# Gated linear attention and a GELU layer on one core: more load buffers, two more pairs through the crossbar, and one dependency in the planner

## The chip, the cores and the metric

The kernel runs on one core of a Trainium2 chip. TensorE multiplies matrices, VectorE (DVE) and ScalarE (ACT) work on elements, GpSimd (POOL) issues the loads here, and SyncE (SP) issues the first loads, the transposes by DMA and the stores. A transpose by DMA goes through the DMA's crossbar and is called that below. The metric is device time in microseconds (us), as the median over runs.

## The reference

For each batch and head (4 batches, 8 heads, 768 tokens, 48 numbers to a head) a state of 48 x 48 is carried over the tokens, and the result goes through a layer with a GELU:

```python
for t in range(S):
    state = alpha[:, :, t, :, None] * state + np.einsum('bhd,bhe->bhde', k[:, :, t], v[:, :, t])
    y[:, :, t] = np.einsum('bhd,bhde->bhe', q[:, :, t], state)
...
x = np.ascontiguousarray(attn_out.transpose(0, 2, 1, 3)).reshape(B * S, H * D)
...
h = x @ w_in                       # 3072 x 384 by 384 x 2048
g = 0.5 * h * (1.0 + np.tanh(c * (h + 0.044715 * h * h * h)))
return (g @ w_out).astype(np.float32)      # 2048 x 384
```

Inputs and output are float32.

## The kernel before

**Tiles.** The tokens are cut into 6 chunks of 128. A chunk of two batches is a *pair*; there are 12, counted here from 0, so pair m is chunk m // 2 and batches 0 and 1 (m even) or 2 and 3 (m odd). The "third pair" of the change is pair 2, the seventh is pair 6, the eighth is pair 7.

**The attention of a pair.** ACT takes the logarithm of alpha (`la`, L294 and L296); TensorE sums it over the tokens with a triangular matrix (`cum`, L313; the sums of the whole chunk, L315); ACT makes `b` = exp(cum), `binv` = exp(-cum) and `bend` from the chunk's sums (L336, L342). DVE makes q' = q·b and k' = k·binv (`qp`, `kp`, L353). q' and k' are transposed into `qkT`: in pairs 0 to 7 on TensorE (L363) with an eviction by DVE or ACT (L381), in pairs 8 to 11 by two crossbar transposes on SP's queue (L401). From `qkT` TensorE makes the products of queries with keys (`at`, L424), DVE masks them (`atm`, L431), and TensorE makes `yps` from the old state (L478) and from `atm` and v (L481). The state takes up k'ᵀv (`kv`, L441; DVE, L463 and L466).

**Between the two halves.** `yps` is copied to `x` by ACT or DVE (L488), and x is transposed into `xT`: in pairs 0 to 6 on TensorE (L495) with a copy by DVE (L499), in pairs 7 to 11 by one crossbar transpose to a batch on SP's queue (L407). There is one `xT` tile to each chunk, six in all.

**The layer.** Block m takes the tokens of pair m: eight steps of first products (`hT`, L507, 6 matmuls each), each followed by a GELU on ACT (L513), then eight groups of second products (`acc`, L526, 4 matmuls each), a copy to `ot` (L538) and a store from SP's queue (L544). These products are one stream with a fixed order; the attention of later pairs is put between them. The logarithms of a pair wait for the last GELU of an earlier block (the table `DECAYS`: pairs 6 and 7 follow block 4, pair 8 follows block 5), because ACT has to load another function table for them.

**What sets the order.** A planner (`Scheduler`) knows every piece of work as a task with a cost, a priority, the tasks it depends on and the buffers it takes. It takes the engine that can go on first, and of that engine's tasks that can start within 60 ns of the earliest the one with the lowest priority number, until all are placed; the instructions are written in that order, and each engine runs its own in order. Attention tasks have lower numbers than the stream, so the stream fills what is left. Where the planner sees TensorE idle for over 300 ns in its first 60 us, it puts in filler products that compute nothing (`idle`, L224). A DMA transpose on SP costs 1.25 us of SP in its table (`turn`) and counts as landed 2.2 us later (`landed`); transposes and stores are counted as one queue (`xbar`). Waits on the chip are set from the tiles that instructions read and write, whatever the planner assumed.

**Buffers.** A task that takes a buffer waits until the users of the one it follows in the ring are done. `BUFS` has 4 load buffers for alpha (`a`), 4 for `q`, 4 for `k`, 2 for float32 v of pairs 0 and 1 (`v`) and 6 for bfloat16 v (`vb`). Loads are issued by POOL in the order of `LOADS` unless a buffer holds one back: weights first, then a, q, k, v of pair after pair. The tag `ca` has one PSUM tile, which `cum` and part of `at` take in turn.

**Pair 2** is worked in two halves (`SPLIT`), one batch each: `parts` gives it two `cum` tasks, whose sums lie in one `ca` tile, and two sets of `b`, `binv`, `bend`. The list `exps` holds these six in order.

Of the kernel before, what the change touches and what calls it, by code (L numbers as in the profile page):

```python
# [5 lines left out]
BF16 = mybir.dt.bfloat16  # L6
F16 = mybir.dt.float16
F32 = mybir.dt.float32
# [128 lines left out]
class _Kernel:  # L137
# [10 lines left out]
             ('a', 1, 0, 1), ('a', 1, 1, 2), ('q', 1, 0, 1), ('k', 1, 0, 1), ('q', 1, 1, 2), ('k', 1, 1, 2))  # L148
    NARROW = (0, 1)

    TURN_QK, TURN_X = (8, 9, 10, 11), (7, 8, 9, 10, 11)

    EV_ACT = (0, 1, 2, 3)

# [1 line left out]

    URGENT = (2,)
    BUFS = dict(ca=1, yk=2, ff=4, la=3, qp=4, kp=4, b8=2, kn=2, qkT=4, atm=6, x=3, ot=5, bend=3, ends=8,
                a=4, q=4, k=4, v=2, vb=6)

    def __init__(self, ctx, tc, q, k, v, alpha, w_in, w_out, out):
        nc = self.nc = tc.nc
        self.tc, self.out = tc, out
        B, H, S, D = q.shape
        self.B, self.H, self.S, self.D = B, H, S, D
        C = self.C = 128
        self.NCH = S // C
        self.src = {"a": alpha, "q": q, "k": k, "v": v}
        self.w_in_dram, self.w_out_dram = w_in, w_out
        self.d_model, self.d_ff = w_in.shape  # L170
        self.NKT, self.NFT = self.d_model // C, self.d_ff // C

        self.const = ctx.enter_context(tc.tile_pool(name="const", bufs=1))
        self.sb = ctx.enter_context(tc.tile_pool(name="sb", bufs=1))
        self.ps = ctx.enter_context(tc.tile_pool(name="ps", bufs=1, space=bass.MemoryType.PSUM))

        const = self.const
        self.ut_h = const.tile([C, C], F16, name="ut_h")
        self.ut = const.tile([C, C], BF16, name="ut")
        self.gate = const.tile([C, 1], F32, name="gate")  # L180
        self.ut_blk = [const.tile([C, C], F16, name=f"ut_blk{i}") for i in range(2)]
        self.blk = const.tile([C, 4], F16, name="blk")
        self.ident = const.tile([C, C], BF16, name="ident")
        self.ones = const.tile([C, 1], F16, name="ones")
        self.zero = const.tile([C, 512], BF16, name="zero")
        self.w_in = [const.tile([C, self.NKT, self.d_ff // 4], BF16, name=f"w_in{i}") for i in range(4)]
        self.w_out = const.tile([C, self.NFT, self.d_model], BF16, name="w_out")
        self.half = const.tile([C, 2], F32, name="half")
        self.state = [[const.tile([C, H // 2, 2 * D], BF16, name=f"st{b}_{i}") for i in range(2)]
                      for b in range(B)]  # L190
        self.ring = {n: [const.tile([C, 2, H, 64], F16 if n == "la" else BF16, name=f"{n}{i}")
                         for i in range(self.BUFS[n])] for n in ("la", "qp", "kp")}
        self.used = {n: 0 for n in self.ring}
        self.xT = [const.tile([C, self.NKT, B, C], BF16, name=f"xT{c}") for c in range(self.NCH)]
        self.NG = 2
        self.gT = [const.tile([C, self.NFT, B * C], BF16, name=f"gT{i}") for i in range(self.NG)]
        self.eng = {"ACT": nc.scalar, "DVE": nc.vector}
# [30 lines left out]
    def load(self, n, c, i, lo=0, hi=2):  # L228

        nc, C, H, D, R = self.nc, self.C, self.H, self.D, self.R  # L230
        u = self.p[c, i]

        def emit(e):
            t = "vb" if n == "v" and u["m"] not in self.NARROW else n
            if t not in u:
                u[t] = self.tile(t, [C, 2, H, D], BF16 if t == "vb" else F32)
            dma = (nc.sync if e == "SP" else nc.gpsimd).dma_start
            src = self.src[n][2 * i + lo:2 * i + hi]
            if u["packed"] and n != "v":
                dma(u[n][:, lo].rearrange("p (o r) d -> p o (r d)", o=2),  # L240
                    src[0, :, c * C:(c + 1) * C].rearrange("h (g r) d -> g h (r d)", r=R))
            else:
                dma(u[t][:, lo:hi].rearrange("t b h d -> t (b h) d"), src.rearrange("b h s d -> s (b h) d")[c * C:(c + 1) * C])  # L243
        return emit
# [159 lines left out]
        return emit  # L404

    def turn_x_dma(self, u, i, c, b):
        return lambda e: self.nc.sync.dma_start_transpose(self.xT[c][:, :, b, :], u["x", i])  # L407

    def attn(self, u, units, apart):
        nc, H, C = self.nc, self.H, self.C  # L410
# [85 lines left out]
        return emit  # L496

    def turned_x(self, u, i, c, b):
        return lambda e: self.copy(e)(self.xT[c][:, :, b, :], u["xT_ps", i])  # L499

    def layer1(self, f, c, lo, hi, nt):
        def emit(e):
            w_in = self.w_in[nt // 4].rearrange("k j (c r) -> k j r c", r=self.NFT // 4)
            h = f["h", c, lo, nt] = self.tile("ff", [self.C, 2, (hi - lo) * self.C], F32, "hT")
            for s in range(2):
                for j in range(self.NKT):
                    self.nc.tensor.matmul(h[:, s], w_in[:, j, nt % 4 + s],  # L507
                                          self.xT[c][:, j, lo:hi].rearrange("p g t -> p (g t)"),
                                          start=j == 0, stop=j == self.NKT - 1, skip_group_check=True)
        return emit  # L510

# [35 lines left out]
    def tasks(self):  # L547
        s = self.s = Scheduler(self.BUFS, self.fill, 60000)
        B, NCH = self.B, self.NCH
# [5 lines left out]
        loads, n, gate, held = {}, 0, [], {}  # L555
# [26 lines left out]
        for step in self.LOADS:  # L582
            if step[0] == "v":
                rows(int(step[1:]), "v")
            elif step[:4] == "gate":
                r, m, j = step[4:].split()
                m, j = int(m), int(j)
# [11 lines left out]
        for m, (c, i) in enumerate(pairs):  # L599
            u, P = self.p[c, i], 100 * m  # L600
# [3 lines left out]
            cums, exps = [], []  # L604
# [28 lines left out]
            if m in self.CUM_FF:  # L633
                cums[0].take("ff", *exps[:3])
                cums[1].take("ff", *exps[3:])
            else:
                cums[0].take("ca", *exps)
            exps[0].take("b8", *qp, *kp)
            if m == 1:
                cums[1].deps.append(ys[1, 0])  # L640
# [5 lines left out]
            vin = [loads["v", m, j] for j in range(2)]  # L646
# [4 lines left out]
            for j in range(2):  # L651
                o, k = P + 10 + 3 * j, kp[j]
# [27 lines left out]
            for j in range(2):  # L680
                b, o, k, ms, turned = 2 * i + j, P + 10 + 3 * j, kp[j], masks[j], turns[j]
                at = ats[m][-1 if m not in self.SINGLE else j]
                if m in self.NARROW:
                    vin[j].deps += turned
                y = s.add("y", {"PE": W["intra"] + (W["inter"] if c else 0)}, P + 20 + j, self.y(u, j, c, b),
                          ms + turned + [vin[j]] + ([states[b, c - 1]] if c else []))
                xc = s.add("x", {"ACT": W["xc_act"], "DVE": W["xc"]}, P + 20 + j, self.x(u, j), [y])
                if m in self.TURN_X:
                    xe = tx = s.add("turn", {"SP": W["turn"]}, P + 22 + j, self.turn_x_dma(u, j, c, b), [xc], xbar=W["xbar_x"], late=W["late_x"] * (m < 7))
                else:  # L690
                    tx = s.add("tx", {"PE": W["tx"]}, P + 22 + j, self.turn_x(u, j), [xc])
                    xe = s.add("xe", {"DVE": W["xe"]}, P + 22 + j, self.turned_x(u, j, c, b), [tx])
                    tx.take("yk", xe)
                y.take("yk", xc)
                xc.take("x", tx)
                users += [at, y]
                ms[0].take("atm", y)
                xts[c, b], ys[b, c] = xe, y
                vs.append(y)
                if c < NCH - 1:  # L700
                    if u["packed"]:
                        tb = s.add("t", {"PE": W["t4"]}, P + 29 + j, self.turn_back(u, j), turned)
                        k = s.add("ev", {"DVE": W["ev4"], "ACT": W["ev4_act"]}, P + 29 + j, self.turned_back(u, j), [tb])
                        tb.take("yk", k)
                        users.append(tb)
                        backs.append(tb)
                    kv = s.add("kv", {"PE": W["kv"]}, P + 30 + j, self.kv(u, j), [k, vin[j]])
                    st = states[b, c] = s.add("st", {"DVE": W["st" if c else "st0"]}, P + 30 + j, self.carry(u, j, c, b),
                                              [kv, end] + ([states[b, c - 1], ys[b, c - 1]] if c else []))
                    kv.take("yk", st)  # L710
                    vs.append(kv)
                    kvs.append(kv)
                    cs.append(st)
# [9 lines left out]
            qp[0].take("qp", *tq)  # L723
            kp[0].take("kp", *tq, *kvs)
            if m in self.NARROW:
                loads["v", m, 0].take("v", *vin)
                vin[0].take("vb", *vs)
            else:
                loads["v", m, 0].take("vb", *vs)
# [115 lines left out]
```

## Time and profile before

| | |
|---|---|
| median of 7 runs | 181.46 us (181.08 to 182.05) |
| the profiled execution | 181.25 us, of which the profile's span is 179.5 us |
| granted TensorE clock | 0.999 of full speed |
| busy: TensorE, ACT, DVE, POOL | 172.9, 130.9, 96.9, 57.6 us |
| loaded from and written to memory | 25.17 MB and 4.72 MB |

Times inside the profile are counted from the start of the span. A group or a row is named by engine, line and tile, written as out<-in. Matmuls overlap: the duration of one is its way through the array, and what a row of them costs the stream is seen from start to start. A wait is put down to the event that came last. "SPq" is SP issuing a DMA; the transfer itself runs on 16 DMA engines and lands later. The forty digits of a row of the overview are the busy tenths of forty equal slices of the span.

### The profile page before, as it was taken

The page shows a single profiled execution, that of the slowest core. Times are in us where ns is not written, and L with a number is a line of the kernel's source. Part 1 is how long each engine was busy: PE and PEld are TensorE (multiplying, and loading weights), DVE is VectorE, ACT ScalarE, POOL GpSimd, SP SyncE. Part 2 cuts the span into 40 slices and gives each one's busy share as a digit, 9 for nine tenths or more (in the row PEclk, how much of TensorE's full clock was granted, in tenths as well). Part 3 has the DMA queues.
Part 4 walks back from the last instruction along what each step waited for, and adds up shares of the span by engine and source line. Part 5 has one row for each costly group of instructions (what it writes and reads, how often), then busy time and mean ns, then how long its engine had stood idle before and what let it go on. Part 6 is the DMA issues. An engine that isn't in the chain of part 4 may idle for free.

```text
span 179.5 us, 4459 instructions
## 1 busy us (share of the span) xinstructions
PE 172.9 (96%) x1860; PEld 136.4 (76%) x1860; DVE 96.9 (54%) x191; ACT 130.9 (73%) x216; POOL 57.6 (32%) x64
## 2 busy tenths in 40 slices
PE   6979999999999999999999999999999999999993
PEld 2557699566896897798698789689688697796972
DVE  6579850145968794596499798199245415000000
ACT  4669778974898678858888757887987984491831
POOL 2397336996646775722721300000000000000000
PEclk9999999999999999999999999999999999999999
DMA  4999999999999999999993736652361270311102
GB/s 121 277 277 212 209 244 233 215 209 208 221 318 187 224 260 197 188 266 201 173 231 97 165 102 104 106 132 54 68 163 45 62 166 26 90 41 47 44 0 88
DMA packets 45957, 28.14 MB, mean 157 GB/s; under 512 B 34545, under 2 KB 42353, under 8 KB 45937
## 3 DMA queue, kind: packets, MB, share of 16 engines
q0 software_dynamic: 26464, 17.70, 59.4%
q1 hardware_dynamic: 19472, 10.16, 21.9%
q8 instruction: 14, 0.23, 0.6%
q14 instruction: 7, 0.05, 0.1%
HBM read 25.17 MB, written 4.72 MB: 167 GB/s over the span
## 4 chain that ended last, share of the span: by engine, by line
PE 90%; DMA 5%; ACT 1%; DVE 1%; SPq 0%; issue 0%; POOL 0%
PE hT L507 35%; PE acc L526 35%; PE at L424 4%; DMA v<-in_v_dram 3%; PE qkT_ps L363 3%; PE yps L481 3%; PE kv L441 2%; PE cum L313 2%; PE yps L478 2%; DMA a<-in_alpha_dram 2%; PE xT_ps L495 1%; PE idle L224 1%; PE cum L281 1%; PE cum L315 1%; PE k_ps L389 1%; ACT vb L324 1%
## 5 line engine op out<-in xcount | busy, mean ns | idle before, releaser
L507 PE MATMUL hT<-xT,w_in 128*128 128x256 bf16 x576 | 69.3, 273 | 0.0
L526 PE MATMUL acc<-w_out,gT 128*128 128x384 bf16 (+1 forms) x400 | 69.1, 320 | 0.0
L513 ACT ACTIVATE gT<-hT 128x512 bf16<-128x512 f32 x96 | 56.7, 597 | 16.5 <-PE hT L507 12.9
L507 PEld LDWEIGHTS <-w_in 128*128 128x128 bf16 x576 | 61.0, 114 | 1.2
L526 PEld LDWEIGHTS <-gT 128*128 128x128 bf16 x400 | 36.7, 98 | 19.2
L431 DVE TENSOR_TENSOR atm<-at,ut 128x512 bf16<-128x512 f32 x48 | 30.3, 682 | 13.2 <-PE at L424 13.1
L353 DVE TENSOR_TENSOR qp<-q,b 128x768 bf16<-128x768 f32 (+1 forms) x15 | 11.9, 794 | 24.9 <-ACT b L342 23.7
L538 ACT COPY ot<-acc 128x384 f32<-128x384 f32 (+1 forms) x18 | 8.2, 458 | 14.1 <-PE acc L526 11.9
L243 POOL DMA_DIRECT2D q<-in_q_dram x11 | 12.2, 1107 | 14.6 <-DVE xT L499 7.1
L243 POOL DMA_DIRECT2D vb<-in_v_dram x11 | 12.1, 1102 | 12.0 <-PE xT_ps L495 6.3
L243 POOL DMA_DIRECT2D a<-in_alpha_dram x11 | 12.2, 1112 | 4.6 <-DMA q<-in_q_dram 1.4
L243 POOL DMA_DIRECT2D k<-in_k_dram x11 | 12.1, 1104 | 4.5 <-DMA w_out<-in_moe_w_out_dram 2.1
L342 ACT ACTIVATE b<-cum 128x768 bf16<-128x768 f32 (+1 forms) x15 | 10.3, 683 | 3.6 <-PE cum L315 2.5
L215 ACT ACT_TABLE_LOAD x9 | 11.5, 1283 | 0.9 <-PEq L829 0.7
L353 DVE TENSOR_TENSOR kp<-k,binv 128x768 bf16<-128x768 f32 (+1 forms) x15 | 11.9, 791 | 0.3 <-DMA k<-in_k_dram 0.3
L513 ACT ACT_TABLE_LOAD x9 | 11.5, 1283 | 0.2
L342 ACT ACTIVATE binv<-cum 128x768 bf16<-128x768 f32 (+1 forms) x15 | 10.2, 680 | 0.0
L381 DVE COPY qkT<-qkT_ps 128x1024 bf16<-128x1024 bf16 (+1 forms) x13 | 8.6, 685 | 2.7 <-PE qkT_ps L363 2.6
L488 DVE CAST x<-yps 128x384 bf16<-128x384 f32 x11 | 6.1, 558 | 7.0 <-PE yps L481 6.9
L224 PE MATMUL idle<-zero 128*128 128x512 bf16 x26 | 8.5, 436 | 1.2 <-DVE half L798 1.2
L463 DVE TENSOR_TENSOR stmp<-kv,st 128x384 f32<-128x384 f32 x16 | 8.8, 551 | 1.2 <-PE kv L441 1.2
L488 ACT CAST x<-yps 128x384 bf16<-128x384 f32 x13 | 6.2, 475 | 4.4 <-PE yps L481 4.4
(63 smaller groups left out, 164.9 us busy)
## 6 DMA issues: line engine op xcount, KB each, us to landing
out_dram<-ot SPq DMA_DIRECT2D x23, 192.0 KB, 2.3
a<-in_alpha_dram POOLq DMA_DIRECT2D x9, 384.0 KB, 11.5
q<-in_q_dram POOLq DMA_DIRECT2D x9, 384.0 KB, 10.9
k<-in_k_dram POOLq DMA_DIRECT2D x9, 384.0 KB, 11.3
vb<-in_v_dram POOLq DMA_DIRECT2D x9, 192.0 KB, 11.6
w_in<-in_moe_w_in_dram POOLq DMA_DIRECT2D x4, 384.0 KB, 9.5
w_out<-in_moe_w_out_dram POOLq DMA_DIRECT2D x4, 384.0 KB, 11.4
a<-in_alpha_dram SPq DMA_DIRECT2D x4, 192.0 KB, 3.6
```

The source lines that it names most:

```text
L215: nc.scalar.add_instruction(mybir.InstLoadActFuncSet(name=nc.get_next_instruction_name(), act_func_set_id=i, engine=mybir.EngineType.Activ ...
L224: self.nc.tensor.matmul(ps, self.zero[:, 0:self.C], self.zero, start=True, stop=True)
L243: dma(u[t][:, lo:hi].rearrange("t b h d -> t (b h) d"), src.rearrange("b h s d -> s (b h) d")[c * C:(c + 1) * C])
L342: self.nc.scalar.activation(u[n].rearrange("t i h d -> t i (h d)")[:, lo:hi], cum, AF.Exp, scale=1.0 if n == "b" else -1.0)
L353: self.nc.vector.tensor_tensor(out, rows, b, op=ALU.mult)
L381: self.copy(e)(t, ps)
L431: self.nc.vector.tensor_tensor(u["atm", i][:, o], u["at", i][o], self.ut[:, None, :].to_broadcast([self.C, self.H // 2, self.C]), op=ALU.mult)
L463: nc.vector.tensor_tensor(s, acc, old, op=ALU.add)
L488: self.copy(e)(x, u["y", i].rearrange("t h d -> t (h d)"))
L507: self.nc.tensor.matmul(h[:, s], w_in[:, j, nt % 4 + s], self.xT[c][:, j, lo:hi].rearrange("p g t -> p (g t)"), start=j == 0, stop=j == se ...
L513: return lambda e: self.nc.scalar.activation(self.gT[c % self.NG][:, nt:nt + 2, lo * self.C:hi * self.C], f.pop(("h", c, lo, nt)), AF.Gelu ...
L526: self.nc.tensor.matmul(f["acc", c, b][:, lo:hi], self.gT[c % self.NG][:, nt, b * self.C:(b + 1) * self.C], self.w_out[:, nt, lo:hi], star ...
```

## The change

- The crossbar also takes q' and k' of pair 7 (two transposes) and x of pair 6 (two transposes). TensorE's transposes and their evictions are left out there.
- `a` has 6 buffers in place of 4, `q` and `k` have 5 in place of 4. The float32 v of pairs 0 and 1 has no buffers of its own any more and takes two of `a`'s.
- There are three `xT` tiles in place of six, used by chunk c modulo 3.
- In the planner, the second `cum` of pair 2 depends on the first half's `b` and `binv`.
- The extra lateness that the planner gave to an x transposed in a pair before 7 is given before 6; no pair that uses the crossbar is under either bound.

```diff
-    TURN_QK, TURN_X = (8, 9, 10, 11), (7, 8, 9, 10, 11)
+    TURN_QK, TURN_X = (7, 8, 9, 10, 11), (6, 7, 8, 9, 10, 11)
...
-                a=4, q=4, k=4, v=2, vb=6)
+                a=6, q=5, k=5, vb=6)
...
-        self.xT = [const.tile([C, self.NKT, B, C], BF16, name=f"xT{c}") for c in range(self.NCH)]
+        self.NX = 3
+        self.xT = [const.tile([C, self.NKT, B, C], BF16, name=f"xT{c}") for c in range(self.NX)]
...
-                u[t] = self.tile(t, [C, 2, H, D], BF16 if t == "vb" else F32)
+                u[t] = self.tile("a" if t == "v" else t, [C, 2, H, D], BF16 if t == "vb" else F32, t)
...
-        return lambda e: self.nc.sync.dma_start_transpose(self.xT[c][:, :, b, :], u["x", i])
+        return lambda e: self.nc.sync.dma_start_transpose(self.xT[c % self.NX][:, :, b, :], u["x", i])
...
+            if m in self.SPLIT:
+                cums[1].deps += exps[:2]
...
-                    xe = tx = s.add("turn", {"SP": W["turn"]}, P + 22 + j, self.turn_x_dma(u, j, c, b), [xc], xbar=W["xbar_x"], late=W["late_x"] * (m < 7))
+                    xe = tx = s.add("turn", {"SP": W["turn"]}, P + 22 + j, self.turn_x_dma(u, j, c, b), [xc], xbar=W["xbar_x"], late=W["late_x"] * (m < 6))
...
-                loads["v", m, 0].take("v", *vin)
+                loads["v", m, 0].take("a", *vin)
```

The other places that name `xT[c]` (L499, L508) become `xT[c % self.NX]` in the same way.

More of the change, by code (lines that the diff above doesn't have):

```diff
@@ L498, in turned_x @@
     def turned_x(self, u, i, c, b):
-        return lambda e: self.copy(e)(self.xT[c][:, :, b, :], u["xT_ps", i])
+        return lambda e: self.copy(e)(self.xT[c % self.NX][:, :, b, :], u["xT_ps", i])
     def layer1(self, f, c, lo, hi, nt):
@@ L507, in emit @@
                     self.nc.tensor.matmul(h[:, s], w_in[:, j, nt % 4 + s],
-                                          self.xT[c][:, j, lo:hi].rearrange("p g t -> p (g t)"),
+                                          self.xT[c % self.NX][:, j, lo:hi].rearrange("p g t -> p (g t)"),
                                           start=j == 0, stop=j == self.NKT - 1, skip_group_check=True)
```

## The prediction

> **What bounds the kernel now.** I read the shares first, then the chain that ended last, then TensorE's own waits, then its order of time at two places, and last the transfers. Pairs are counted from 0: the eighth pair is pair 7, the seventh pair 6, the third pair 2.
>
> ```profile
> PE 172.9 (96%) x1860; PEld 136.4 (76%) x1860; DVE 96.9 (54%) x191; ACT 130.9 (73%) x216; POOL 57.6 (32%) x64
> PE   6979999999999999999999999999999999999993
> DMA  4999999999999999999993736652361270311102
> PE 90%; DMA 5%; ACT 1%; DVE 1%; SPq 0%; issue 0%; POOL 0%
> ```
>
> TensorE is busy in every slice from the fourth to the last but one, at a granted clock of 0.999. Asked for TensorE's waits from 20 us to the end, the trace has one:
>
> ```profile
> PE cum L313 <- ACT binv L342: 0.3, 1, 0.3
> ```
>
> So a microsecond taken out of TensorE's stream comes off the end, and the one stall is the second. In the order of time it looks so:
>
> ```profile
> 34.57 0.24 PE L315 MATMUL cum<-ones,la 128*128 128x1 f16 x4
> 34.67 0.81 PE L526 MATMUL acc<-w_out,gT 128*128 128x384 bf16 x4
> 35.77 0.32 PE L313 MATMUL cum<-la,ut_h 128*128 128x384 f16 x1 [0.29 <-ACT binv L342]
> ```
>
> Four products `acc` fill 0.65 us (0.162 us start to start), so they end issuing at 35.32; the next instruction starts at 35.77. Counted by starts the hole is 0.45 us (the 0.29 leaves out the modelled tail of the last product). The second sum of pair 2 waits for `binv` of the first half: both halves lie in one `ca` tile, and the planner did not know of that wait.
>
> **The change part by part.** *q', k' of pair 7 by crossbar.* Away go 16 transposes on TensorE; the chain, in order of time, has them at 99.82, and the transposes of pair 6's x just ahead (start, duration, count):
>
> ```profile
> 97.53 0.17 PE xT_ps L495 x3
> ...
> 99.00 0.17 PE xT_ps L495 x3
> ...
> 99.82 0.89 PE qkT_ps L363 x16
> ```
>
> The sixteen are 0.89 us of TensorE; two evictions on DVE (1.29 us at 100.30) go too; no row has another engine held up by them. In come two DMA transposes on SP's queue, each 1.24 us of issue; DVE, ACT and POOL get nothing new.
>
> *x of pair 6 by crossbar.* Away go 2 x 3 transposes, 2 x 0.17 = 0.34 us of TensorE, and two copies on DVE (0.36 each). In come two more SP transposes of 1.24 us. SP has room: between its store issues at 90.27 and 103.14 it issues nothing, and the four need about 5.0 us.
>
> *The order of pair 2's sums.* The planner now puts the second sum after the first half's `b` and `binv`. Worked by hand from its cost table (taken for the order alone), one more `acc` group (0.65 us) goes ahead of the sum and nothing else changes place: the transposes of pair 2 still follow three groups later. The second sum then starts at 35.32 + 0.65 = 35.97, after `binv` has ended at 35.71. The hole of 0.45 us goes. What is late next: the second half's `b`, `binv`, q', k' each move 0.20 later (k' done at 38.02 in place of 37.82); its transposes stood at 38.43 (q) and 38.65 (k) and would come at 37.98 and 38.20. They still find their input, by 0.2 us. Sums, evictions and the first products of block 2 at 47.11 then all follow 0.45 earlier; the copy of x they wait for follows TensorE's order too.
>
> *Buffers.* POOL's loads of q, k, a come up to one or two pairs earlier; v of the first two pairs takes two of the six `a` buffers, as many in all as before (4 + 2), so up to pair 5 the loads keep their order. After that the gain is no time by itself: after 20 us POOL alone waits for loads (a wait of q' on DVE at 58.8 is put down to one, but ended with `b`, at 58.73), and the cover is wide (a of pair 5 landed at 54.2, used at 70.7). What it moves is the end of the load traffic:
>
> ```profile
> 88.74 1.16 POOL L243 DMA_DIRECT2D q<-in_q_dram  x1 [0.58 <-DVE qp L353]
> 89.89 1.15 POOL L243 DMA_DIRECT2D k<-in_k_dram  x1
> 98.11 1.15 POOL L243 DMA_DIRECT2D q<-in_q_dram  x1 [7.07 <-DVE xT L499]
> 99.36 1.15 POOL L243 DMA_DIRECT2D k<-in_k_dram  x1
> ```
>
> The last q and k waited for a buffer until pair 7's q' was made; with five buffers they wait for pair 6's, at about 88 to 89. The loads then run without holes: 24 are to come once v of pair 5 has landed at 59.3; the next 17 landed in 27.4 us, 1.6 each, so they end near 98, where before the load landed at 97.3 was followed by a hole, and by the last two at 102.9 and 104.4. The three `xT` tiles in place of six reuse a tile three chunks later; its readers ended more than 40 us before, cost 0.
>
> *Do the four transposes land in time?* This is the open price. Shifted by the 0.45: first x of pair 6 is ready at 95.33 and issues then; q' is ready at 97.25; the second x (ACT, 97.71) waits behind q' on SP and issues at 98.6; k' (DVE no longer copies x between q' and k': done at 98.2) issues at 99.9, behind it. The nearest rows are the same four kinds in the same order, one pair later:
>
> ```profile
> 107.17 1.28 SPq L407 DMA_TRANSPOSE xT<-x  x1
> 108.56 1.24 SPq L401 DMA_TRANSPOSE qkT<-qp  x1
> 109.89 1.24 SPq L407 DMA_TRANSPOSE xT<-x  x1
> 111.22 1.26 SPq L401 DMA_TRANSPOSE qkT<-kp  x1
> ```
>
> They landed 2.4, 3.5, 4.3 and 3.8 us after issue began. So x lands at 97.8 and 102.9, q' at 100.8, k' at 103.7. Needed: block 6's first product stood at 105.32; less 0.45, less 1.23, less about 0.6 if `at` of pair 7 now comes behind it, it wants x at 103.0; `at` (L424) wants k' about 0.65 later, at 103.7. Both just fit. Anything later stalls TensorE at once: the queue is in order, and behind that product wait the gelus on ACT and all of block 6.
>
> The loads are the unknown. A store on the same queue took 5.3 us at 90.27 with loads in flight, 1.9 to 2.9 at 103 to 107 with few, and 6.2 to 9.5 between 44 and 80. Bounds for the stall: 0 (quiet rows) and 4 us (the second x takes 8.4, the store at 57.92, and lands at 107). It can't be below 0, as TensorE does not wait there now. I take 0.3, near the quiet end: by 98.6 the loads are landed or nearly so, and only the first x meets them.
>
> *Two rules from the skill.* The row: one crossbar transpose of q' carries eight 128x128 blocks and lands in 2.7 us (117 to 121), while its blocks hold TensorE 55 ns each. The Trainium skill, "VectorE: DVE Perf Modes", Rules for kernel authors, says to transpose 128x128 on TensorE where PSUM will do, and its table of three paths has 390 ns there and 1309 ns on the crossbar. Read serially that is an estimate of 22 blocks at 0.92 us more, 20 us lost and a time near 201. Here TensorE is the bound and the crossbar's time lies beside it, so the row decides. Second row: the store of 90.27, 5.3 us. The skill's "DMA: Bandwidth & Descriptors", Queues, rings and completion order, has each DMA engine turn between queues packet by packet; then a transpose would not wait out the loads and the stall would be 0, 1.7 us saved. The row has the store behind loads issued before it; I keep 0.3.
>
> **The sum.** 0.89 + 0.34 + 0.45 - 0.30 = 1.38 us off the profiled execution, 181.25 us (span 179.5 and 1.75 around it), so 179.9; it stands 0.21 under the median of 181.46, which becomes 180.1.
>
> **The rivals.** *Slower: the second x of pair 6 is stuck behind the loads.* Place: block 6's first product. It decides once x lands after 103.0 + 1.68 = 104.7, a latency over 6.1 us from 98.6. For it: stores took 6.2 to 9.5 us under full load, and the added buffers keep the loads going to about 98. Against: by 98.6, when that x issues, the loads have ended by my count. At 8.4 us: 4.0 lost, 1.7 won, 183.8; at 7 us, 182.4.
>
> *No difference.* The same wait at 5.7 to 6.4 us: 1.3 to 2.0 lost, about 181.4.
>
> *Only the transposes count.* The hole at 35 us is refilled: the last gap before block 2 (one filler product at 46.56) shows TensorE was short of work there, and if x of pair 2 keeps its time, 46.76, the 0.45 comes back as filler or wait. Against: that x hangs on TensorE's own order, which moves as a whole. Then 1.23 - 0.3 = 0.93: 180.5.
>
> *The change does more than needed and nothing stalls:* 1.68 off, 179.8; with the lower runs 179.5.
>
> **How the numbers follow.** Forecast (both gains, stall 0 to 0.7: 179.8 to 180.5): 0.60. Only the transposes, or a stall of 0.7 to 1.3 (180.5 to 181.1): 0.20. No difference: 0.09. Slower: 0.11. A measurement tells about 0.2% (0.36 us) from nothing. Faster is the first two, 0.80. The range runs from 179.5 to 181.5; the likeliest case alone 179.5 to 180.5.
>
> **What would show it.** Right: 112 transposes of q', k' on TensorE in place of 128, 36 of x in place of 42; by the crossbar 12 of x in place of 10, and 10 of q', k' in place of 8; no wait of `cum` for `binv`; POOL done before 92; block 6's first product near 103.0. Wrong: a wait of `hT` or `at` for a transfer between 102 and 108, latencies over 5 us there, or new filler products before 47 us, which would mean that the planner's order moved elsewhere too.

## The result, and the profile after

| | before | after |
|---|---|---|
| median | 181.54 us (45 runs) | 180.82 us (17 runs) |
| ratio of after to before | | 0.9952, interval 0.9939 to 0.9966 |
| the profiled execution (its span) | 181.25 us (179.5) | 180.74 us (179.0) |
| first product of block 1 to first product of block 11 | 139.38 us | 138.65 us |

The kernel is faster by 0.72 us, where 1.38 was forecast. The last row of the table is read from the two traces, and it is the measure for all traces below. It leaves out the start, since block 0's first product comes at 16.0 to 16.6 us in most traces and at 18.7 and 18.9 in two. It also leaves out the end, and there the change costs 0.24 us: from block 11's first product to the end of the span it is 13.62 us before and 13.86 after. The work of TensorE in that stretch is the same. The difference comes behind the last store's landing, from where the span goes on for 0.98 us before and 1.21 after. There SP has two semaphore events in the kernel before and six in the kernel after, 0.06 us apart. In all fourteen traces of this case two such events go with 0.96 to 0.98 us, six with 1.21 to 1.23, eight with 1.34 to 1.36.

So the two spans differ by 0.51 us (0.73 less 0.24, and 0.03 at the start), and that the 0.73 of the last row is so near the 0.72 of the medians is in part luck. Lines of the kernel after are numbered one higher than before, and two or three higher towards the end of the file.

The page of the kernel after, in the shares, the tenths and the chain that ended last:

```profile
PE 172.5 (96%) x1838; PEld 135.7 (76%) x1838; DVE 95.1 (53%) x187; ACT 131.3 (73%) x216; POOL 57.8 (32%) x64
...
PE   6999999999999999999999989999999999999992
...
DMA  4999999999999999999999970353270360401102
...
PE 88%; DMA 8%; DVE 1%; ACT 1%; SPq 0%; issue 0%; POOL 0%
```

TensorE has 22 instructions less, as forecast (16 and 6 transposes; 112 and 36 are left). DMA is at 9 for some slices longer and then drops. In the chain its share rose from 5% to 8%, by a line that was not there before: `DMA qkT<-kp`, 3%. TensorE's waits from 20 us to the end say the same; the wait of `cum` for `binv` is gone and another has come:

```profile
PE at L425 <- DMA qkT<-kp: 0.8, 1, 0.8
```

TensorE in order of time, at the two places that the prediction named:

```profile
34.54 0.24 PE L316 MATMUL cum<-ones,la 128*128 128x1 f16 x4
34.64 1.46 PE L527 MATMUL acc<-w_out,gT 128*128 128x384 bf16 x8
35.94 0.33 PE L314 MATMUL cum<-la,ut_h 128*128 128x384 f16 x1
...
103.02 0.82 PE L508 MATMUL hT<-xT,w_in 128*128 128x256 bf16 x6
104.68 0.62 PE L425 MATMUL at<-qkT 64*128 64x128 bf16 x16 [0.84 <-DMA qkT<-kp]
```

Pair 2's second sum starts at 35.94 with no wait. Block 6's first product starts at 103.02; its six matmuls start 0.109 us apart, so the next instruction could start at 103.68, and `at` of pair 7 starts at 104.68. Counted by starts, TensorE stands still for 1.0 us (the 0.84 leaves out the modelled tail). So 0.45 + 0.34 + 0.89 = 1.68 us of work and idling went, and 1.0 came back: 0.68 between block 1 and block 11, where the two traces differ by 0.73. With the 0.24 at the end 0.44 is left.

The four issues on SP, in order of time, are where they were expected:

```profile
95.33 1.27 SPq L408 DMA_TRANSPOSE xT<-x  x1
97.29 1.23 SPq L402 DMA_TRANSPOSE qkT<-qp  x1
98.61 1.21 SPq L408 DMA_TRANSPOSE xT<-x  x1
99.91 1.26 SPq L402 DMA_TRANSPOSE qkT<-kp  x1
```

They landed at 101.0, 101.84, 102.27 and 104.64. POOL issued the last two loads well ahead of them:

```profile
88.80 1.15 POOL L244 DMA_DIRECT2D q<-in_q_dram  x1 [0.66 <-DVE kp L354]
90.71 1.15 POOL L244 DMA_DIRECT2D k<-in_k_dram  x1 [0.76 <-DVE qkT L382]
```

The last load landed at 100.65. The question of the experiments is why k' took 4.73 us after its issue.

**Theory L**, the prediction's: the loads are still in flight and delay what is issued beside them. **Theory F**, the rival, came from the DMA view of the stretch from 102 to 104.6 us (40 slices of 0.065 us: busy tenths and GB/s of all engines; below, the queues with packets, MB and share; the hardware queue carries SP's transposes and stores, the software queue POOL's loads):

```profile
DMA  9999999999900000000000000101011069999989
GB/s 295 268 280 288 532 260 284 268 443 363 189 0 0 0 0 0 0 0 0 0 4 8 8 8 8 12 8 12 8 12 24 0 236 378 378 378 378 378 162 299
...
q1 hardware_dynamic: 909, 0.38, 113.3%
q8 instruction: 1, 0.02, 2.6%
```

No load is left on the software queue here, and yet for some 1.3 us (102.7 to 104.0) nearly nothing moves. Just before, at 102.27, one packet of 16 KB starts on an "instruction" queue and takes 1.09 us: by the queue's name, the core fetches code. The single packets tell more. A transpose of q' or k' here ends with 32 packets of 4 bytes. Of those of k', 30 start between 102.53 and 102.63 and the last two at 103.97. In between, 22 packets of 256 bytes run one after another from 103.345 to 103.947, nearly all at 35 to 56 ns in place of 18, and the first of them starts 14 ns before the fetch ends (103.359). The store's packets, issued behind k', stand from 102.6 to 104.1. So a sixteenth of k' seems to wait until the fetch is through, and all else behind it; that is a reading, which the experiments test. The Trainium skill, "Runtime: NRT & Kernel Launch", section Instruction fetch mechanics, says that code reaches an engine in blocks of 16 KB, 256 instructions, by a DMA queue of its own; the queue of this profile with 14 packets and 0.23 MB fits that size. What such a block does to other transfers, the runs have to show.

### The profile page after: what moved, and what is told of

Read it like the earlier page. It is cut to its first block, busy times and chain, and to the rows that moved or that the text cites. A ratio compares the mean times of both kernels' runs of the same rounds, so it can differ in the third digit from the quotient of the medians.

```text
span 179.0 us, 4421 instructions
## 1 busy us (share of the span) xinstructions
PE 172.5 (96%) x1838; PEld 135.7 (76%) x1838; DVE 95.1 (53%) x187; ACT 131.3 (73%) x216; POOL 57.8 (32%) x64
## 4 chain that ended last, share of the span: by engine, by line
PE 88%; DMA 8%; DVE 1%; ACT 1%; SPq 0%; issue 0%; POOL 0%
PE hT L508 35%; PE acc L527 33%; PE at L425 4%; DMA v<-in_v_dram 3%; PE qkT_ps L364 3%; PE yps L482 3%; DMA qkT<-kp 3%; PE kv L442 2%; PE yps L479 2%; PE cum L314 2%; DMA a<-in_alpha_dram 2%; PE xT_ps L496 1%; PE idle L225 1%; PE cum L282 1%; PE cum L316 1%; PE k_ps L390 1%
## 5 line engine op out<-in xcount | busy, mean ns | idle before, releaser
L508 PE MATMUL hT<-xT,w_in 128*128 128x256 bf16 x576 | 69.0, 273 | 0.0
L508 PEld LDWEIGHTS <-w_in 128*128 128x128 bf16 x576 | 61.1, 113 | 1.2
L467 DVE TENSOR_TENSOR st<-stmp,ends 128x384 bf16<-128x384 f32 x16 | 8.9, 558 | 0.6
```

The source lines that it names most:

```text
L467: nc.vector.tensor_tensor(new.rearrange("f p (o d) -> f (p o) d", o=2), acc.rearrange("f p (o d) -> f (p o) d", o=2), ends, op=ALU.mult)
L508: self.nc.tensor.matmul(h[:, s], w_in[:, j, nt % 4 + s], self.xT[c % self.NX][:, j, lo:hi].rearrange("p g t -> p (g t)"), start=j == 0, st ...
```

## The experiments

### Moving the code fetches

TensorE's filler products at the start of the kernel compute nothing. Written as four products of 128 columns in place of one of 512, they add 78 products early (156 instructions, with their weight loads) and little time, and everything that TensorE fetches later is fetched at another moment. If the fetch makes k' late, k' comes in time; if the loads do, nothing changes.

```diff
-                self.nc.tensor.matmul(ps, self.zero[:, 0:self.C], self.zero, start=True, stop=True)
+                for j in range(4):
+                    self.nc.tensor.matmul(ps[:, j * 128:(j + 1) * 128], self.zero[:, 0:self.C], self.zero[:, 0:128], start=True, stop=True)
```

**After with these fillers:**

> The changed kernel, with each filler product of 512 columns written as four of 128 columns: the same columns, 78 more products, 156 more instructions on TensorE before 47 us. Theory F (instruction fetch): TensorE's code comes in blocks of 16 KB by DMA, one in some 11 us; the one at 102.27 us held one DMA engine for 1.09 us while k' of pair 7 was on the crossbar, and all engines waited, so k' landed at 104.6 and L425 stalled 1.0 us. With 156 instructions more ahead of it the fetch comes about 6.8 us earlier, at 95 to 97, k' lands at about 103.1, the stall is under 0.2 us and the time 0.7 to 1.0 us below the changed kernel's (179.8 to 180.1; ratio to before 0.990 to 0.993). Theory L (loads): the transposes are late because load traffic runs to 100.6; then k' still lands at 104.4 to 104.8, the stall stays at 0.8 to 1.0 us and the time at 180.8.

Measured: 180.35 us, 0.9934 of before (0.9915 to 0.9952); block 1 to block 11 takes 137.75 us, 0.90 less than after. The fetch begins at 95.91, where theory F had put it (95 to 97). k' is issued at 100.47 and lands 2.74 us later, and `at` doesn't wait. The DMA view from 100.4 to 103.3 us has no instruction queue:

```profile
GB/s 106 208 187 226 212 208 138 42 0 1 0 0 0 0 0 0 0 35 159 261 290 290 297 290 293 286 290 282 297 293 195 57 4 106 148 275 339 339 381 360
...
q1 hardware_dynamic: 1556, 0.50, 72.0%
```

k' moves between 101.6 and 102.8 without a break. This speaks for F, with one weakness: in this run the loads ended at 99.4, before k' was issued, while after had them until 100.65.

**Before with these fillers**, as a control:

> Control: the kernel before with the filler products split in four. Nothing on TensorE's path waits for a transfer there, so both theories expect the time of before, ratio 0.9985 to 1.0015. Theory F also expects the fetch of 112.19 to come near 105.4 and the transposes issued at 109.89 and 111.22 to land about 1 us sooner than their 4.3 and 3.8 us; theory L expects them as they were.

Measured: 1.0040 of before (1.0022 to 1.0059), where the expectation was no change: the fillers cost something there, so what they win above isn't their own cheapness. In the profile the fetch that fell at 112.19 moved to 105.7, and the transposes at 109.84 and 111.14, which took 4.3 and 3.8 us in before, took 2.5 and 2.8. But another fetch moved onto 118.4, where q' of pair 9 was under way: it took 3.7 us (2.7 in before), k' was issued behind it at 119.81 in place of 119.44, and `at` waited:

```profile
PE at L425 <- DMA qkT<-kp: 0.2, 1, 0.2
```

From block 1 to block 11 the trace takes 139.62 us, 0.24 more than before. The profiled execution was the fastest of its runs (181.43, the median is 182.36), so what most runs lost beyond that, some 0.5 us of the 0.73 that the ratio gives, is in no trace and stays open.

**The same kernels again**, one profiled execution each, to separate the loads from the fetch: after twice, after with the fillers once more, and with fillers of two products of 256 columns, which should bring the fetch to another moment again.

```diff
-                self.nc.tensor.matmul(ps, self.zero[:, 0:self.C], self.zero, start=True, stop=True)
+                for j in range(2):
+                    self.nc.tensor.matmul(ps[:, j * 256:(j + 1) * 256], self.zero[:, 0:self.C], self.zero[:, 0:256], start=True, stop=True)
```

> The changed kernel itself, a second look at its trace. Theory F (code fetch): the fetch comes at 102.0 to 102.8 counted from a start like the first look's, k' of pair 7 is on the queue then, and L425 waits 0.5 to 1.2 us. Theory L (loads): the wait goes with the landing of the last load: about 1 us if that is at 100.5 or later, none if it is before 99. Theory B (both are needed): a wait only where k' is still being moved when the fetch begins, and that is so where the last load lands late.

> The changed kernel itself, a third look; expected as for the second: F a wait of 0.5 to 1.2 us whatever the loads do, L a wait that goes with the last load's landing alone, B a wait only where k' is still being moved at the fetch.

> The kernel with filler products in four, a second look: its fetch comes at about 96 and the next at about 108. F and B expect no wait of L425 for k' over 0.2 us, even if the last load lands at 100.5 or later; L expects about 1 us in that case.

> The changed kernel with each filler product in two of 256 columns: 52 more instructions on TensorE, a fetch about 2.3 us earlier, at 100, when q' or the second x are on the crossbar. F: they land about 1 us later than without, k' follows at 103.2 to 104.0, and L425 waits 0 to 0.4 us. L: as the changed kernel, by the last load's landing. B: no wait over 0.4 us.

The four executions took 183.22, 181.04, 179.87 and 180.08 us. In the first, block 0's first product came 2.65 us later than in after and the granted clock was 0.50 from 13.6 to 17.0 us, so its total says nothing; from there on the clock is whole and its transfers can be read. The traces, in order of the fetch's place:

| kernel | fetch begins | last load landed | k' issued | k' takes | `at` stands (page's wait) |
|---|---|---|---|---|---|
| after, fillers in four | 95.91 | 99.4 | 100.47 | 2.74 | 0 |
| the same again | 96.77 | 99.76 | 99.94 | 2.80 | 0 |
| after, fillers in two | 100.13 | 98.9 | 100.13 | 3.57 | 0 |
| after | 102.27 | 100.65 | 99.91 | 4.73 | 0.8 |
| after again (second execution) | 102.41 | 100.4 | 100.34 | 4.58 | 0.7 |
| after again (first execution) | 104.43 | 99.87 | 102.57 | 4.53 | 0.7 |

The last row decides. All loads had landed 2.7 us before k' was issued, and k' was still 1.8 us late. The DMA view of that run from 102.5 to 107.2 us (40 slices of 0.118 us) and its wait:

```profile
GB/s 135 224 220 196 48 1 0 0 0 0 13 183 283 292 292 285 423 272 227 53 65 288 118 0 0 0 0 2 9 9 9 9 11 13 144 353 418 292 249 294
...
q1 hardware_dynamic: 1867, 0.62, 86.3%
q8 instruction: 1, 0.02, 1.8%
```

```profile
PE at L425 <- DMA qkT<-kp: 0.7, 1, 0.7
```

It is the same picture as in after, without loads: k' moves at full rate, the rate falls to 0 and then to 9 GB/s, and k' ends late. In the single packets 30 of the 32 end marks start between 104.68 and 104.85 and two at 106.40, and the 22 late packets begin at 105.767, 14 ns before the fetch ends (105.781). The other execution of after has 103.586 and 103.600, again 14 ns. With the fetch elsewhere, in the two executions with fillers in four, all 32 marks start within 0.2 us. So theory L falls as the reason of this wait, and theory B with it, for k' waited here though no load was late. In fillers in two the fetch lies at the beginning of k' and on q' and the second x (4.62 and 3.68 us), and k' lands at 103.71, 0.3 us before `at` starts. Three executions of after with the fetch on k' all wait; three with the fetch moved don't.

Over all fourteen traces of this case, the transposes that were issued after the last load had landed, sorted by whether a packet of an instruction queue was in flight at any time between issue and landing. There are two such queues, one with packets of 16 KB and one with a few of 8 KB:

| | no fetch: number, us from issue to landing | with a fetch: number, us from issue to landing, median |
|---|---|---|
| x, one batch | 63: 2.28 to 2.38 | 79: 2.28 to 4.34, 2.81 |
| q' | 37: 2.70 to 2.79 | 19: 2.75 to 3.96, 3.36 |
| k' | 50: 2.72 to 2.95 | 10: 2.76 to 4.53, 3.36 |

Of 150 transposes without a fetch none is late. With one, some are on time, such as the k' of 2.76 us whose fetch began after its end marks (in the version with room, below).

### The parts, one at a time

**The order of pair 2's sums alone, in before:**

```diff
+            if m in self.SPLIT:
+                cums[1].deps += exps[:2]
```

> The kernel before with the one new dependency of pair 2's second sum alone. The prediction's step: the hole of 0.45 us before the sum goes and nothing comes back, 0.45 us faster (ratio 0.9975), first product of block 2 at 46.65. Rival (the hole is refilled): block 2 starts at 47.1 as before, ratio 1.000.

Measured: 181.13 us, 0.9970 (0.9954 to 0.9986); block 1 to block 11 takes 138.93, 0.45 us less. TensorE in order of time has the eight `acc` products in place of four and no wait:

```profile
34.93 1.46 PE L526 MATMUL acc<-w_out,gT 128*128 128x384 bf16 x8
36.22 0.33 PE L313 MATMUL cum<-la,ut_h 128*128 128x384 f16 x1
```

From block 2 on the distances from block to block are those of before. The hole isn't refilled later: the rival that said so falls.

**The order, the buffers and x of pair 6**, q' and k' of pair 7 staying on TensorE:

```diff
-    TURN_QK, TURN_X = (7, 8, 9, 10, 11), (6, 7, 8, 9, 10, 11)
+    TURN_QK, TURN_X = (8, 9, 10, 11), (6, 7, 8, 9, 10, 11)
```

> The changed kernel with q', k' of pair 7 back on TensorE; x of pair 6 by crossbar, buffers and order kept. By the terms of the sum 0.45 + 0.34 = 0.79 us below before with no stall (ratio 0.9956): block 6's first product is wanted at 104.5 and the second x, issued at about 97.8, lands at 101 to 102.5 even with the loads. Rival (a transpose beside loads or a code fetch always costs TensorE): a wait of hT for xT over 0.3 us and a ratio over 0.997.

Measured: 181.24 us, 0.9983 (0.9959 to 1.0007), too close to 1 for the runs to tell; the trace has 138.56, 0.82 us less, where 0.45 + 0.34 = 0.79 was the sum. Its end is 0.36 us longer than before's, so 0.46 is left of it, beside 0.31 by the ratio. The second x was issued at 98.2 and took 2.6 us, and no `hT` waits.

**The order, the buffers and q', k' of pair 7**, x of pair 6 staying on TensorE:

```diff
-    TURN_QK, TURN_X = (7, 8, 9, 10, 11), (6, 7, 8, 9, 10, 11)
+    TURN_QK, TURN_X = (7, 8, 9, 10, 11), (7, 8, 9, 10, 11)
```

> The changed kernel with x of pair 6 back on TensorE; q', k' of pair 7 by crossbar, buffers and order kept. By the terms 0.45 + 0.89 = 1.34 us below before if nothing stalls (ratio 0.9926). k' goes out one transpose earlier, at about 98.7, but the planner then also wants it earlier: L425 comes at about 102.7, with loads running to 100.6 and the code fetch at about 102. Theory F expects k' between 102.3 and 104.0 and a stall of 0 to 1.3 us (ratio 0.9926 to 0.998); theory L, with two transposes fewer behind the loads, expects it by 102.5 and no stall.

Measured: 180.84 us, 0.9954 (0.992 to 0.9987); the trace has 138.01, 1.37 us less, against 0.45 + 0.89 = 1.34. Without the two x ahead of it on SP, k' is issued at 99.19, 0.7 us earlier than in after, and with a fetch in it (101.84) it lands at 102.39, early enough. With its longer end (0.37 us) 1.0 us of the gain is left, beside 0.84 by the ratio. By the traces this kernel is ahead of after by 0.64 us up to block 11, as after gives back 1.0 in the wait and saves 0.34 by the x transposes. The ratios (0.9954 and 0.9952) don't show that lead; the interval of this one is 0.6 us to either side.

**The buffers alone:**

```diff
-    TURN_QK, TURN_X = (7, 8, 9, 10, 11), (6, 7, 8, 9, 10, 11)
+    TURN_QK, TURN_X = (8, 9, 10, 11), (7, 8, 9, 10, 11)
...
-            if m in self.SPLIT:
-                cums[1].deps += exps[:2]
```

> The changed kernel with TensorE's transposes and the order of before: the buffers and the three xT tiles alone. The prediction's step: no time by themselves, ratio 0.9985 to 1.0015; the last load lands at about 100.6 in place of 104.4. Rival (earlier loads help or hurt by contention): a ratio outside 0.998 to 1.002.

Measured: 181.70 us, 0.9993 (0.9971 to 1.0015); the trace has 139.39 in place of 139.38. By themselves they do nothing that runs or trace could tell.

**Everything but the buffers:**

```diff
-                a=6, q=5, k=5, vb=6)
+                a=4, q=4, k=4, v=2, vb=6)
...
-                u[t] = self.tile("a" if t == "v" else t, [C, 2, H, D], BF16 if t == "vb" else F32, t)
+                u[t] = self.tile(t, [C, 2, H, D], BF16 if t == "vb" else F32)
...
-                loads["v", m, 0].take("a", *vin)
+                loads["v", m, 0].take("v", *vin)
```

> The changed kernel with the load buffers of before (a 4, q 4, k 4, v 2): crossbar and order kept. Loads then pause from about 97 and only the last q and k run beside the transposes, to 103 or 104. Theory L: the first x of pair 6 lands at about 98 in place of 101 and k' at 103.0 to 103.7, the stall falls to 0 to 0.3 us and the time to about 180.0 to 180.2. Theory F: TensorE's instructions are the same in number, the fetch comes at 102.3 again, k' lands at 104 or later, the stall stays at 0.7 us or more, time 180.5 to 181.0.

Measured: 186.57 us, 1.0251 (1.0212 to 1.029), slower by 2.5% where both theories had 181 or less, further off than any other expectation here. Without the buffers the last loads wait for pair 7's q', as in before, and now meet the transposes. POOL's issues in order of time:

```profile
97.75 1.15 POOL L244 DMA_DIRECT2D q<-in_q_dram  x1 [7.06 <-DVE qp L354]
98.89 1.15 POOL L244 DMA_DIRECT2D k<-in_k_dram  x1
```

The second x of pair 6, issued at 98.73, takes 6.3 us, k' of pair 7 8.3 us, and the two loads take 6.2 and 8.8 us (4.8 and 5.1 in before). Not all of this is the loads and transposes alone: a code fetch at 104.85 to 106.12 (theory F had put it at 102.3) lies on k' and on the load of k as well. The second x landed at 105.03 and the load of q at 103.94, so these two owe nothing, or next to nothing, to the fetch. TensorE's waits:

```profile
PE at L425 <- DMA qkT<-kp: 2.5, 1, 2.5
PE hT L508 <- DMA xT<-x: 1.8, 1, 1.8
```

And with the second wait the engine becomes slower. In three stretches (length, then busy time and instructions of PE, PEld, DVE, ACT, POOL, granted clock, DMA share, GB/s):

```profile
98.00:103.00 5.00, 5.00 (x45) 3.18 (x44) 3.88 (x8) 4.70 (x7) 2.04 (x2) 1.00 0.93 172
103.00:109.00 6.00, 1.73 (x20) 1.25 (x20) 0.98 (x3) 1.20 (x2) 0.00 (x0) 0.77 1.22 165
109.00:113.00 4.00, 4.00 (x31) 2.88 (x28) 3.94 (x7) 0.82 (x2) 0.00 (x0) 0.50 0.47 124
```

In the second TensorE does 1.73 us of work in 6; in the third it has work all the time, at a granted clock of 0.50. Against after, block 1 to block 11 takes 5.79 us more, and the trace accounts for it. Counted by starts, TensorE stands still for 1.93 us before block 6's first product and for 2.67 before `at`, 4.60 in place of 1.0. The granted clock is 0.50 from 106.25 to 113.07. In that time the 16 products `at` take 0.97 us in place of 0.56, the 8 products `kv` 0.62 in place of 0.35, and the next 15 products `hT` 3.15 in place of 1.64 (0.213 from start to start in place of 0.109): 2.19 together. 3.60 + 2.19 = 5.79.

So theory L's mechanism is real where loads and transposes lie side by side, and the buffers keep them apart: after issued its last loads at 88.80 and 90.71. The Trainium skill, "DMA: Bandwidth & Descriptors", section Rules for kernel authors, says, in a rule about transposes that corrupt each other's data, that a transpose beside ordinary DMAs needs nothing. That is said of the data; for time these rows have 6.3 us for an x against 2.28 to 2.38 undisturbed.

### A version with room for the fetch

TensorE's queue is in order and the planner puts `at` of pair 7 where it expects k' to land, 2.2 us after its issue ends. If the fetch can't be steered, `at` can be put later: the planner counts q' and k' of pair 7 as landing 1.4 us later, and first products of block 6 go ahead.

```diff
-                    xbar=W["xbar_qk"]
+                    xbar=W["xbar_qk"], late=1400 * (m == 7)
```

> The changed kernel, and the planner counts q' and k' of pair 7 as landed 1.4 us later, so that L425 of pair 7 stands two groups of block 6's products further back, wanted at about 105.3. If the gain that is missing (1.38 forecast, 0.72 measured) is the wait for k' and nothing else, the stall of 1.0 us goes, and the time is 179.8 to 180.0 (ratio 0.990 to 0.9925). Rival (the lost time is a delay of pair 7 that is paid later anyway): a new wait behind it, at pair 7's x or at L425 of pair 8, and 180.6 or more.

Measured: 180.13 us (179.93 to 180.5), 0.9911 of before (0.9879 to 0.9942), just above the 179.8 to 180.0 that was expected. Block 1 to block 11 takes 137.73, 1.65 us less than before, where the sum without a stall is 1.68. TensorE in order of time:

```profile
103.38 0.82 PE L508 MATMUL hT<-xT,w_in 128*128 128x256 bf16 x6
104.03 0.50 PE L442 MATMUL kv<-vb,kp 128*128 128x96 bf16 x8
104.38 1.47 PE L508 MATMUL hT<-xT,w_in 128*128 128x256 bf16 x12
105.78 0.62 PE L425 MATMUL at<-qkT 64*128 64x128 bf16 x16
```

TensorE waits for nothing after 20 us. In this trace k' took 2.76 us (issued at 100.28; the fetch began at 102.66, when its end marks were already done) and would have been in time in after's order too. So this trace doesn't show that the new order bears a fetch. That is read from its room: `at` is issued 5.5 us after k', and no k' of the three executions of after took over 4.73. It has the lowest median of the timed versions; its interval against before touches that of after (0.9939 to 0.9966) at its upper end.

## Why the prediction was right, and where it was off

- **q', k' of pair 7 (0.89 us) and x of pair 6 (0.34): right** up to block 11. With the order, the traces of the parts give 1.37 and 0.82 for sums of 1.34 and 0.79.
- **The hole before pair 2's second sum (0.45): right**, in time (35.94 for 35.97), in amount (0.45 alone), and in that one more `acc` group takes its place and nothing else moves.
- **Buffers no time by themselves: right** (0.9993). That they move the end of the load traffic forward was right as well, but to 100.65 and not to 98. The first x and q' met the loads for it and landed at 101.0 and 101.84, where 97.8 and 100.8 were forecast; nothing wanted them so early, so it cost nothing. What the move is worth in company has no term in the sum: without it the same change loses 2.5%.
- **The room of `at` and of block 6's first product: right.** x was wanted at 103.0 and landed at 102.27, the product started at 103.02; `at` was wanted at 103.7 and could have started at 103.68.
- **The stall of 0.3: off, and the term that missed.** It measured 1.0. The step was "Do the four transposes land in time?". The prices of 2.4, 3.5, 4.3 and 3.8 us came from four transposes of the next pair, read as a property of x and q' following each other; three of them carried a code fetch, q' one of 8 KB at 109.48 and the second x and k' one of 16 KB at 112.19. In the control that moved the second fetch, x and k' took 2.5 and 2.8, and q', whose fetch stayed, still 3.35. The step then left the remaining doubt to the loads. In its place the runs showed an undisturbed k' of 2.72 to 2.95 and a fetch that adds up to 1.8 to it. The prediction had named a wait of `at` for a transfer between 102 and 108 as a sign of being wrong, and this sign came. Without the fetch k' of after would have landed near 103.1, an estimate: its 30 marks were done at 102.63, and with the fillers in four the last mark at 102.75 meant a landing at 103.21. That is before 103.68, so nothing would have stalled; of the 104.64, the loads and the queue give at most the 0.4 between 102.7 (2.8 us from its issue) and 103.1, the fetch the other 1.5.
- **The end of the program: a term at nothing.** Four more semaphore events on SP cost 0.24 us there. What each of them is for, no trace says; that they come with the added transposes is all that the runs show (two in every kernel without, six or eight in every kernel with).
- **The sum:** 1.68 less 1.0 less 0.24 is 0.44; the two spans differ by 0.51, the medians by 0.72. That 0.68, without the end, lies so near the 0.72 is luck: the profiled execution of before was 0.29 under its median, that of after 0.08. The time, 180.82, lies in the case "a stall of 0.7 to 1.3", the forecast's second.
- **The rivals.** "The second x is stuck behind the loads" has the right mechanism and the wrong kernel: the second x landed at 102.27, before its limit, and what the rival describes happened when the buffers were taken away. "Nothing stalls" (179.8) is what the version with room comes near, 180.13. "Only the transposes count" fell with the order alone. "No difference" fell with the result.

## What to carry to other kernels

Before a transfer gets a price from another row, look at what else the queues carried in that row, the instruction queue too; and where an in-order engine waits for a landing on time to a tenth of a microsecond, give it two microseconds of other work first, because a fetch can fall on it, and an edit that changes the number of instructions ahead moves the fetch. A change that costs nothing and wins nothing alone can be what the rest stands on: here the buffers. So take a change apart both ways, each part alone and everything but that part. And where a time is taken between two marks in a trace, ask what the change does outside them: here 0.24 us at the end.

## What the runs showed of the hardware

- **A code fetch holds up transposes by DMA.** One 16 KB packet on an instruction queue took 0.88 to 1.71 us, and a crossbar transpose that was under way then could land up to 2 us later: x 2.28 to 2.38 us without and up to 4.34 with, k' 2.72 to 2.95 without and up to 4.53 with. The 8 KB packets did it too: q' 3.52 in before, 2.70 to 2.79 without. In three traces fifteen sixteenths of k' ended on time; the rest began 14 ns before the fetch ended, each time, and the store behind k' stood until they were through. That the fetch sits on one of the 16 DMA engines, whose share of k' comes after it, fits all of this; the trace doesn't name the engine of a packet, so that part is a reading.
- **Products that compute nothing move the fetches.** 78 more at the start (156 instructions) brought the fetch from 102.27 to 95.91, and block 1 to block 11 took 0.90 us less.
- **Loads and transposes side by side can slow each other:** an x 6.3 us in place of 2.3, the load of q 6.2 in place of 4.8, with no fetch on either but for the last 0.2 us of the x. It isn't so each time: in the first of the executions again the first x lay beside the last load and took 2.38.
- **In the run without the buffers TensorE's granted clock fell to 0.50**, from 106.25 to 113.07, after it had stood still for 1.93 us and again from 105.72 on. From 108.39 it had work, so that is 4.7 us of work at half the pace. The one wait of 1.0 us in after was followed by nothing of the kind: its clock stays at 1.00 until 177.8.
